# An attention and two mixtures of experts on one core: weights prepared later, gate terms on another engine, a state without zero blocks

## The chip, the cores and the metric

The kernel runs on 1 core of a Trainium2 chip. The metric is device time in microseconds (us): 711.42, the median of 3 runs (710.65 to 711.84). Five engines work in parallel, each through its own instructions in a fixed order: PE (TensorE, matrix products), DVE (VectorE), ACT (ScalarE), POOL (GpSimd) and SP (SyncE, which here only issues transfers). An instruction that waits holds up all that stand behind it on its engine.

## The reference, cut to what matters

```python
for t in range(S):                       # attention: B=2, H=8, S=768, D=40
    m_new  = max(f[t] + m, i[t])
    f_stab, i_stab = exp(f[t] + m - m_new), exp(i[t] - m_new)
    C = f_stab * C + i_stab * outer(v[t], k[t])
    n = f_stab * n + i_stab * k[t]
    y[t] = sigmoid(o[t]) * (C @ q[t]) / max(abs(n @ q[t]), 1)
x = y laid out as 1536 rows of 320
noisy = x @ w_gate + log1p(exp(x @ w_noise)) * noise       # 8 experts
out[r] = sum over r's two best experts of weight * (relu(x[r] @ w1[e]) @ w2[e])
final = sum over 4 experts of p[:, e] * (relu(out @ v1[e]) @ v2[e])
```

## The kernel before, in words

The attention goes in 12 chunks of 128 positions, 6 for each of the two batches. For a chunk, `o_S` (L346) makes the scores `sp` of keys and queries, `o_decay` (L323) makes a matrix `A` of decays on PE (`dp`), takes its exponent on ACT and masks it on POOL, `o_M` multiplies the two on DVE, and `o_AV` (L413) multiplies by the values into `hp`, on top of what `o_inter` (L402) put there from the running state `C` of the chunks before. ACT copies `hp` to `hs`, `o_tp` transposes it into `tp`, and `o_x` (L429) normalizes it on DVE and multiplies by the sigmoid of the output gate into `x`. `o_xp` transposes `x` again (`xp`, copied to `xt`), and `o_lg` makes the routing logits. The state is advanced by `o_Cg` (POOL, decay `gb`), `o_U` (PE, `up`, from the weighted keys `kw`) and `o_Cu` (DVE). `C` holds 4 pairs of heads in blocks of 105 columns: the two heads of a pair stand on rows 0 to 39 and 64 to 103, and the other two blocks are zero.

What `A` needs of the two gates is made along the whole sequence in four parts, chunk 0, chunk 1, chunks 2 and 3, chunks 4 and 5 (`PARTS`): `gates` (L246) does the scans on DVE, `gates_terms` (L260) forms the factors `tk` and `tq` of the decay's exponent, and `gates_turn` transposes the weights `awr`. `LFh` and `ash` are rounded copies that ACT makes for it. `sigmoid(b)` (L282) takes the sigmoid of a batch's output gates in one ACT instruction between two loads of ACT's function tables.

For each batch `route` (L479) places each row's two experts, in two halves (4 and 2 chunks), some 30 small DVE instructions each: `rh` and `oh` are the factors of the products `pt` (L551) that fill the table `tok`, from which POOL gathers (L616) the rows `xe` of an expert from `Xall` in DRAM. Then `moe1` works through the experts (hidden layer L207, second layer L221), and `moe2` does the four experts of the second mixture over all rows. A weight is loaded (`raw`, 4 buffers, L173) and split into a high part on ACT (L187) and a low part on DVE (L188), five quarters of `w1` and five of `w2` ahead of use.

The order on each engine comes from a scheduler that places an instruction when its model of the chip says the inputs are there; `tc.issue_after` puts instructions behind a given one. So splits written far down in the program are placed wherever an engine looked free. `PLAN1` says which pieces are written one after the other: `A` a piece of the attention (four a chunk), `r` and `q` a piece of the two halves of the routing, `l` a load of a weight, `w` a split and a load, `g` the second batch's sigmoid, `X` the first gathers, `P` the first expert's rows.

Of the kernel before, what the change touches and what calls it, by code (L numbers as in the profile page):

```python
# [65 lines left out]
def body(ctx: ExitStack, tc: tile.TileContext, d, o, dbg=None):  # L66
# [159 lines left out]


# [5 lines left out]
    fi_load(slice(0, 1))  # L233
# [26 lines left out]
    def gates_terms(part):  # L260

        n = PARTS[part]
        nc.scalar.copy(LFh[:, n], LF[:, n])
        nc.scalar.copy(ash[:, n], asr[:, n])
        nc.vector.tensor_scalar(flat(LF, n), flat(LF, n), low, keys, ALU.mult, ALU.add)
        nc.vector.scalar_tensor_tensor(flat(LF, n), flat(LFh, n).bitcast(F32), qsel, flat(LF, n), ALU.mult, ALU.add)
        nc.vector.tensor_scalar(flat(asr, n), flat(asr, n), key, sums, ALU.mult, ALU.add)
# [99 lines left out]
    def o_kw(i):  # L367
        b, c = divmod(i, NC)
        if c < NC - 1:
            kw = at2.tile([P, H, D], F32, name="kw")  # L370
            nc.vector.tensor_mul(kw, st[i]["kv"][:, :, 0:D], w_t[:, c, b * H : (b + 1) * H].unsqueeze(2).to_broadcast([P, H, D]))
            st[i]["kw"] = kw

    def o_Cg(i):
        c = i % NC
        if 0 < c < NC - 1:
            for j in range(2):
                r, e = slice(64 * j, 64 * j + 40), slice(64 * j, 64 * j + 41)
                nc.gpsimd.tensor_mul(Cs[1 - c % 2][r, :, e], Cs[c % 2][r, :, e], st[i]["gb"][r, :, P - 1 : P].to_broadcast([40, 4, 41]))

    def o_U(i):
        if i % NC < NC - 1:
            t = st[i]
            up = psum([104, 4, 41], "up")
            for p in range(4):
                for j in range(2):
                    nc.tensor.matmul(up[64 * j : 64 * j + 40, p, :], t["kw"][:, 4 * j + p, :], t["kv"][:, 4 * j + p, D:], start=True, stop=True)
            t["up"] = up

    def o_Cu(i):  # L390
        c = i % NC
        if c < NC - 1:
            up = st[i]["up"]
            for j in range(2):
                r = slice(64 * j, 64 * j + 40)
                cs = Cs[1 - c % 2][r, :, 64 * j : 64 * j + 41]
                if c == 0:
                    st[i]["cu"] = nc.vector.tensor_copy(cs, up[r]).ins
                else:
                    nc.vector.tensor_add(cs, up[r], cs)  # L400
# [44 lines left out]
    def o_xp(i):  # L445
# [485 lines left out]
    def splits():  # L931
        for _ in range(NQ):
            w_split()
            w_load()
            yield

    def follow(plan, b, first):
        r, q, f, w = route(b, 0), route(b, 1), routed_(b), splits()
        for group in plan.split():
            for t in group:  # L940
# [121 lines left out]
```

## Time and profile before

| | us |
|---|---|
| median of 3 runs | 711.42 |
| the profiled execution | 714.27 |
| its span | 712.5 |
| PE busy | 679.9 (95%) |
| DVE busy | 379.2 (53%) |
| ACT busy | 248.3 (35%) |
| POOL busy | 108.3 (15%) |
| start of the scores of chunks 1, 2, 3, 6, 7 | 18.14, 41.97, 51.85, 70.83, 79.09 |
| first rows of an expert on PE | 112.33 |

The span runs from the first to the last instruction; the remaining 1.8 us of the profiled execution lie around it. The busy share of PE counts an instruction for as long as it takes at the clock that it was granted.

### The profile page before, as it was taken

How to read it: one execution, taken by the hardware profiler on the slowest of the kernel's cores; microseconds unless marked ns; L12 is line 12 of the kernel's file. 1: busy time of each engine (PE TensorE's matmuls, PEld its weight loads, DVE VectorE, ACT ScalarE, POOL GpSimd, SP SyncE). 2: the span in 40 equal slices, each digit the busy share in tenths (PEclk: the TensorE clock that was granted, in tenths of full speed). 3: DMA queues.
4: the chain of work that ended last, by engine and by line, in shares of the span. 5: the costliest groups of instructions: out<-in, count | busy, mean ns of one | idle time of the engine just before them, and what ended most of it. 6: DMA issues, size and time to landing. Idle time of an engine off the chain costs nothing.

```text
span 712.5 us, 11304 instructions
## 1 busy us (share of the span) xinstructions
PE 679.9 (95%) x4448; PEld 618.6 (87%) x4448; DVE 379.2 (53%) x834; ACT 248.3 (35%) x439; POOL 108.3 (15%) x168
## 2 busy tenths in 40 slices
PE   7588889999999999999999999999999999999997
PEld 3367668999899999999989899898998998989987
DVE  7887876888465745747865525413344124332131
ACT  3638323554353534544541314202233023121120
POOL 4554433102222101014114000000000000000000
PEclk8569769999999999999999999999999999999999
DMA  8667433556465454467663003200031001001011
GB/s 259 193 181 211 132 76 88 172 181 199 131 193 158 139 163 126 133 180 246 199 193 100 1 1 104 59 1 1 19 107 38 1 1 37 1 1 38 1 37 40
DMA packets 36433, 73.78 MB, mean 104 GB/s; under 512 B 7576, under 2 KB 14744, under 8 KB 36376
## 3 DMA queue, kind: packets, MB, share of 16 engines
q1 hardware_dynamic: 33752, 64.16, 30.1%
q0 software_dynamic: 2624, 8.85, 4.3%
q8 instruction: 37, 0.61, 0.4%
q14 instruction: 20, 0.16, 0.1%
HBM read 64.07 MB, written 8.92 MB: 102 GB/s over the span
## 4 chain that ended last, share of the span: by engine, by line
PE 85%; DVE 7%; DMA 4%; ACT 1%; issue 1%; SPq 0%; ACTq 0%; DVEq 0%
PE z L207 24%; PE z L221 24%; PE s L207 13%; PE s L221 11%; DMA raw<-w 2%; PE sp L353 2%; PE hp L418 2%; PE lp L461 1%; PE s L217 1%; DVE w1lo L188 1%; DMA raw<-v 1%; PE hp L411 1%; DMA fi<-fi 1%; PE pa L630 1%; DVE hh L225 1%
## 5 line engine op out<-in xcount | busy, mean ns | idle before, releaser
L224 ACT ACTIVATE hh<-z 128x512 fp32r<-128x512 f32 x96 | 57.1, 600 | 190.7 <-PE z L207 189.4
L221 PE MATMUL z<-w2hi,hh 128*128 128x320 f32 x384 | 118.5, 309 | 0.0
L221 PE MATMUL z<-w2hi,hl 128*128 128x320 f32 x384 | 118.3, 308 | 0.0
L221 PE MATMUL z<-w2lo,hh 128*128 128x320 f32 x384 | 118.3, 308 | 0.0
L207 PE MATMUL z<-x2h,w1hi 128*128 128x512 f32 x288 | 112.4, 390 | 0.0
L221 PE MATMUL s<-w2hi,hh 128*128 128x320 f32 x448 | 107.8, 313 | 2.5 <-issue 1.2
L225 DVE SCALAR_TENSOR_TENSOR hl<-z,hh 128x512 fp32r<-128x512 f32 x96 | 65.7, 690 | 80.9 <-ACT hh L224 80.9
L207 PE MATMUL z<-x2h,w1lo 128*128 128x512 f32 x288 | 96.6, 389 | 0.0
L188 DVE TENSOR_TENSOR w2lo<-raw,w2hi 128x640 fp32r<-128x640 f32 x60 | 50.3, 841 | 68.3 <-ACT w2hi L187 64.3
L207 PE MATMUL s<-xh,w1hi 128*128 128x256 f32 (+1 forms) x288 | 85.3, 313 | 0.0
L221 PEld LDWEIGHTS s<-w2hi,hh 128*128 128x128 f32 x448 | 76.7, 188 | 4.3 <-issue 1.9
L207 PE MATMUL z<-x2l,w1hi 128*128 128x512 f32 x192 | 74.8, 390 | 0.0
L188 DVE TENSOR_TENSOR w1lo<-raw,w1hi 128x768 fp32r<-128x768 f32 x60 | 58.7, 979 | 29.4 <-ACT w1hi L187 28.9
L187 ACT CAST w2hi<-raw 128x640 fp32r<-128x640 f32 x60 | 43.8, 731 | 87.0 <-PE s L217 23.9
L221 PEld LDWEIGHTS z<-w2lo,hh 128*128 128x128 f32 x384 | 72.1, 188 | 0.6
L221 PEld LDWEIGHTS z<-w2hi,hh 128*128 128x128 f32 x384 | 72.1, 188 | 0.5
L221 PEld LDWEIGHTS z<-w2hi,hl 128*128 128x128 f32 x384 | 72.1, 188 | 0.0
L207 PE MATMUL s<-xh,w1lo 128*128 128x256 f32 (+1 forms) x288 | 70.6, 309 | 0.0
L221 PE MATMUL s<-w2lo,hh 128*128 128x320 f32 x224 | 69.2, 309 | 0.0
L187 ACT CAST w1hi<-raw 128x768 fp32r<-128x768 f32 x60 | 50.3, 838 | 48.7 <-PE s L207 23.8
L207 PEld LDWEIGHTS z<-x2h,w1lo 128*128 128x128 f32 x288 | 54.1, 188 | 11.3
L207 PEld LDWEIGHTS z<-x2h,w1hi 128*128 128x128 f32 x288 | 54.0, 188 | 10.8
(204 smaller groups left out, 1003.4 us busy)
## 6 DMA issues: line engine op xcount, KB each, us to landing
raw<-w SPq DMA_DIRECT2D x44, 384.0 KB
raw<-w SPq DMA_DIRECT2D x44, 320.0 KB
raw<-v SPq DMA_DIRECT2D x16, 384.0 KB
raw<-v SPq DMA_DIRECT2D x16, 320.0 KB
kv<-kv SPq DMA_DIRECT2D x12, 324.0 KB
Yd<-ys SPq DMA_DIRECT2D x8, 320.0 KB
kp<-kT SPq DMA_DIRECT2D x12, 208.0 KB
qt<-qT SPq DMA_DIRECT2D x12, 208.0 KB
```

Source lines behind the costliest of these rows:

```text
L187: nc.scalar.copy(hi, raw)
L188: nc.vector.tensor_sub(lo, raw, hi.bitcast(F32))
L207: nc.tensor.matmul(out_ps, l, r, start=(i == 0), stop=(i == len(seq) - 1))
L217: nc.tensor.matmul(yp, both[f], r[:, k], start=(f == 0 and i == 0), stop=(f == NF - 1 and i == 1))
L221: nc.tensor.matmul(yp, l, r, start=(f == 0 and i == 0), stop=(f == NF - 1 and i == 2))
L224: nc.scalar.activation(hh, src, AF.Relu)
L225: nc.vector.scalar_tensor_tensor(hl, src, 0.0, hh.bitcast(F32), ALU.max, ALU.subtract)
L353: nc.tensor.matmul(sp[g][:, j, :], t["kp"][r, j, :], t["qt"][r, j, :], start=True, stop=True)
L411: nc.tensor.matmul(hp[:, p, :], Cs[c % 2][:, p, :], t["qg"][:, p, :], start=(p == 0), stop=False)
L418: nc.tensor.matmul(hp[64 * j : 64 * j + 41, p, :], t["kv"][:, 4 * j + p, D:], t["A"][:, 4 * j + p, :], start=False, stop=(p == 3))
L461: nc.tensor.matmul(lp, xts[i % 2][:, k, :], wgn[:, k, : 2 * E1], start=(k == 0), stop=(k == 2))
L630: nc.tensor.transpose(pk[k][:, c], xe[:r, s, k * P : (k + 1) * P], ident[:r, :r])
```

## The change

The change has seven parts. The loads `l` and the splits `w` of `PLAN1` are put behind the newest transfer of `kv` (SP), exponent of a decay (ACT) and product with `A` (DVE) that were written before them, and the plan moves them later. The first sigmoid is put behind chunk 1's exponents, which no longer wait for it; the terms of gate part 2 are put behind it instead. In parts 1 to 3 of the gates, two DVE operations and the product `tq` of POOL become ACT instructions (`tq` in four pieces of 128 columns). `C` loses its zero blocks: one instruction where there were two in `o_Cg` and `o_Cu`, and eight small matrix products instead of four in `o_inter`. The narrow half of `xt` is copied by ACT instead of DVE. The gates' load is cut after two chunks instead of one. The routing gets one more break before the products `pt`, and the gathers `X` come one group sooner.

```diff
-PLAN1 = "A A A A A A Al A Al A Ag Al A Al A A Ar Ar Aw Ar Ar Aw Ar Ar Aqr Aqr Aq Aqr Aqw Aq Aq qwX Aq AF A AF A F P"
+PLAN1 = "A A A A A A A A Al A Ag Al A Al A Al Ar Ar Ar Ar Awr Ar Awr Ar Aqr Aqr Awq Aq Awq Aq Aq Aq qX Aq AF A F A F P"
+    front = {}
+    def behind():
+        stack = ExitStack()
+        for ins in front.values():
+            stack.enter_context(tc.issue_after(ins))
+        return stack
-    fi_load(slice(0, 1))
+    fi_load(slice(0, 2))
...
-        nc.vector.tensor_scalar(flat(LF, n), flat(LF, n), low, keys, ALU.mult, ALU.add)
+        if part == 0:
+            nc.vector.tensor_scalar(flat(LF, n), flat(LF, n), low, keys, ALU.mult, ALU.add)
+        else:
+            nc.scalar.activation(flat(LF, n), flat(LF, n), AF.Identity, scale=low, bias=keys)
...
-        eng = nc.vector if part == 0 else nc.gpsimd
         for c in range(n.start, n.stop):
...
+            else:
+                for j in range(4):
+                    nc.scalar.activation(tq[:, c, j], LF[:, c], AF.Identity, scale=head[:, j : j + 1])
...
-        C = at.tile([104, 4, 105], F32, name=f"C{i}")
+        C = at.tile([104, 4 * 41 + 24], F32, name=f"C{i}")
...
-            for j in range(2):
-                r, e = slice(64 * j, 64 * j + 40), slice(64 * j, 64 * j + 41)
-                nc.gpsimd.tensor_mul(Cs[1 - c % 2][r, :, e], Cs[c % 2][r, :, e], st[i]["gb"][r, :, P - 1 : P].to_broadcast([40, 4, 41]))
+            nc.gpsimd.tensor_mul(state(1 - c % 2), state(c % 2), st[i]["gb"][:, :, P - 1 : P].to_broadcast([104, 4, 41]))
...
-                nc.tensor.matmul(hp[:, p, :], Cs[c % 2][:, p, :], t["qg"][:, p, :], start=(p == 0), stop=False)
+                for j in range(2):
+                    r, m = slice(64 * j, 64 * j + D), 41 if j else 64
+                    nc.tensor.matmul(hp[64 * j : 64 * j + m, p, :], Cs[c % 2][r, 41 * p : 41 * p + m], t["qg"][r, p, :], start=(p == 0), stop=False)
...
-        nc.vector.tensor_copy(xt[0:DR, 2], xp[0:DR, 2])
+        nc.scalar.copy(xt[0:DR, 2], xp[0:DR, 2])
...
             nc.vector.tensor_mul(rh[:, 1, c], in_col[:, c], place[...])
         yield
+        yield
         pt = psum([P, 2, E1 * NCOL], "pt")
...
-    exps = sigmoid(0, st[-1]["exp"])
-    with tc.issue_after(exps):
-        for op in ("D0", "D1", "G", "S"):
-            do(op, 1)
+    for op in ("D0", "D1", "G", "S"):
+        do(op, 1)
+    exps = sigmoid(0, front["act"])
...
-    with tc.issue_after(last):
+    with tc.issue_after(last), tc.issue_after(exps):
         last = gates_terms(2)
...
     def splits():
         for _ in range(NQ):
-            w_split()
+            with behind():
+                w_split()
+                w_load()
+            yield
+
+    def behind_load():
+        with behind():
             w_load()
-            yield
```

On ACT, between the weights of chunk 1 (`w_t`) and the first weights of gate part 2, this stands in the kernel before (`x_91` is batch 0's output gate, `dp_330` and `dp_334` the decays of chunk 1):

```order
L280 ACTIVATE w_t<-pt_300 128x16
L284 ACT_TABLE_LOAD
L286 ACTIVATE x_91<-x_91 128x1920
L420 COPY hs<-hp_312 105x512
L288 ACT_TABLE_LOAD
L333 ACTIVATE A<-dp_330 128x512
L333 ACTIVATE A<-dp_334 128x512
L343 ACTIVATE gb<-gp_338 104x512
L263 CAST LFh<-LF 128x256
L264 CAST ash<-asr 128x256
L280 ACTIVATE w_t<-pt_373 128x16
L187 CAST w1hi<-raw 128x768
```

And from the exponents of chunk 1 on in the changed kernel (`tq` x8 are the factors of chunks 2 and 3):

```order
L350 ACTIVATE A<-dp_329 128x512
L350 ACTIVATE A<-dp_333 128x512
L360 ACTIVATE gb<-gp_337 104x512
L301 ACT_TABLE_LOAD
L303 ACTIVATE x_91<-x_91 128x1920
L305 ACT_TABLE_LOAD
L272 CAST LFh<-LF 128x256
L273 CAST ash<-asr 128x256
L277 ACTIVATE LF<-LF,mix,kind 128x256
L282 ACTIVATE asr<-asr,mix,kind 128x256
L297 ACTIVATE w_t<-pt_381 128x16
L289 ACTIVATE tq<-LF,head 128x128 x8
```

The exponents and `gb` of chunk 1 now stand before the sigmoid and its table loads, six or more new instructions before the exponents of chunk 2, and no split of a weight.

On DVE, in the second half of batch 0's routing up to `rh`, this stands before:

```order
L535 TENSOR_REDUCE sf_1198<-tmp_1197 128x4
L579 RECIPROCAL mx<-mx 128x6
L359 TENSOR_TENSOR A<-sp_1213,A 128x512
L534 TENSOR_TENSOR tmp_1197<-sel,sl_1143 128x32
L543 TENSOR_TENSOR in_col_1205<-count,sf_1198 128x128
L535 TENSOR_REDUCE sf_1198<-tmp_1197 128x4
L359 TENSOR_TENSOR A<-sp_1214,A 128x512
L541 TENSOR_TENSOR oh_1203<-count,sf_1198 128x512
L544 TENSOR_SCALAR rh_1204<-in_col_1205,place 128x128
L547 TENSOR_TENSOR rh_1204<-in_col_1205,place 128x64 x2
```

And in the changed kernel, in the same place:

```order
L596 TENSOR_TENSOR lk<-lk,mx 128x12
L188 TENSOR_TENSOR w2lo<-raw,w2hi 128x640
L555 TENSOR_REDUCE sf_1234<-tmp_1233 128x4
L598 TENSOR_TENSOR mx<-lk 128x6
L188 TENSOR_TENSOR w2lo<-raw,w2hi 128x640
L554 TENSOR_TENSOR tmp_1233<-sel,sl_1179 128x32
L563 TENSOR_TENSOR in_col_1241<-count,sf_1234 128x128
L555 TENSOR_REDUCE sf_1234<-tmp_1233 128x4
L599 TENSOR_SCALAR mx<-mx 128x6
L564 TENSOR_SCALAR rh_1240<-in_col_1241,place 128x128
L561 TENSOR_TENSOR oh_1239<-count,sf_1234 128x512
L567 TENSOR_TENSOR rh_1240<-in_col_1241,place 128x64 x2
```

Two of the low parts of `w2` now stand among the routing's instructions; the two products with `A` went ahead of this piece.

On PE, around the last product of that table (`up_1259`, `dp_1269` and `dp_1273` belong to chunks 10 and 11), before:

```order
L551 LDWEIGHTS oh_1203
L551 MATMUL pt_1239<-rh_1204,oh_1203 128x64
L387 MATMUL up_1259<-kv,kw 40x41 x7
L332 MATMUL dp_1269<-tq,tk 128x512
L332 MATMUL dp_1273<-tq,tk 128x512
L461 MATMUL lp_1282<-wgn,xt_189 128x16 x3
L426 MATMUL tp_1291<-ident,hs 128x105 x4
```

And now:

```order
L407 MATMUL up_1274<-kv,kw 40x41
L349 MATMUL dp_1284<-tq,tk 128x512
L349 MATMUL dp_1288<-tq,tk 128x512
L481 MATMUL lp_1297<-wgn,xt_189 128x16 x3
L572 LDWEIGHTS oh_1239
L572 MATMUL pt_1303<-rh_1240,oh_1239 128x64
```

The products for `up`, `dp` and `lp` stood behind those of the table and now stand ahead of them.

## Rows read from the trace of the kernel before

**Rows 1.** the page, its head and the engines' busy time
```profile
span 712.5 us, 11304 instructions
...
PE 679.9 (95%) x4448; PEld 618.6 (87%) x4448; DVE 379.2 (53%) x834; ACT 248.3 (35%) x439; POOL 108.3 (15%) x168
```

**Rows 2.** timeline of PE: start, us, engine, line, form, count [idle before <-releaser]
```profile
18.14 2.08 PE L353 MATMUL sp<-qt,kp 40*128 40x128 f32 x16
...
25.89 0.80 PE L332 MATMUL dp<-tq,tk 32*128 32x512 f32 x2 [2.98 <-POOL tq L272]
...
28.01 0.79 PE L332 MATMUL dp<-tq,tk 32*128 32x512 f32 x2
32.90 0.45 PE L279 MATMUL pt<-ident,awr 128*128 128x128 f32 x1 [4.09 <-DVE awr L257]
...
36.38 1.58 PE L418 MATMUL hp<-A,kv 128*41 128x128 f32 x16
41.14 0.69 PE L449 MATMUL xp<-ident,x 128*128 128x128 f32 x2 [3.17 <-DVE x L439]
...
41.97 2.08 PE L353 MATMUL sp<-qt,kp 40*128 40x128 f32 x16
...
51.85 1.16 PE L353 MATMUL sp<-qt,kp 40*128 40x128 f32 x16
```

**Rows 3.** timeline of ACT to 62 us
```profile
11.36 0.30 ACT L263 CAST LFh<-LF 128x128 fp32r<-128x128 f32 x1 [1.66 <-DVE LF L254]
...
14.23 1.81 ACT L286 ACTIVATE x<-x 128x1920 f32<-128x1920 f32 x1
...
18.84 1.28 ACT L288 ACT_TABLE_LOAD   x1
...
24.08 0.83 ACT L187 CAST w1hi<-raw 128x768 fp32r<-128x768 f32 x1 [1.69 <-DMA raw<-w]
...
30.06 1.08 ACT L333 ACTIVATE A<-dp 128x512 f32<-128x512 f32 x2
```

**Rows 4.** timeline of DVE to 62 us
```profile
32.67 2.03 DVE L188 TENSOR_TENSOR w1lo<-raw,w1hi 128x768 fp32r<-128x768 f32 x1
...
52.60 0.94 DVE L188 TENSOR_TENSOR w1lo<-raw,w1hi 128x768 fp32r<-128x768 f32 x1
...
55.30 0.33 DVE L400 TENSOR_TENSOR C<-up,C 40x164 f32<-40x164 f32 x1
...
58.56 0.28 DVE L453 COPY xt<-xp 64x128 f32<-64x128 f32 x1 [1.29 <-ACT xt L452]
```

**Rows 5.** timeline of POOL
```profile
24.69 2.40 POOL L272 TENSOR_TENSOR tq<-LF,head 128x512 fp32r<-128x512 f32 x2 [0.43 <-DVE LF L266]
...
104.07 1.18 POOL L616 DMA_INDIRECT xe<-Xall,tok  x1 [6.14 <-DVE wdense L584]
```

**Rows 6.** windows: stretch, us, each engine busy (instructions), clock, DMA share, GB/s
```profile
40.00:50.00 10.00, 8.86 (x60) 7.25 (x62) 8.29 (x18) 3.82 (x8) 3.89 (x5) 0.54 0.81 240
50.00:60.00 10.00, 10.00 (x129) 8.05 (x126) 7.11 (x20) 7.39 (x12) 5.61 (x7) 0.94 0.75 227
...
80.00:90.00 10.00, 7.18 (x102) 5.81 (x98) 9.80 (x41) 3.15 (x8) 3.94 (x5) 0.93 0.46 139
90.00:100.00 10.00, 8.01 (x68) 6.42 (x64) 8.11 (x38) 2.93 (x7) 3.56 (x5) 0.73 0.38 95
```

**Rows 7.** timeline of PE from 59 us
```profile
70.35 0.44 PE L449 MATMUL xp<-ident,x 128*128 128x128 f32 x2 [1.99 <-DVE x L439]
...
70.83 1.42 PE L353 MATMUL sp<-qt,kp 40*128 40x128 f32 x16
...
79.09 1.16 PE L353 MATMUL sp<-qt,kp 40*128 40x128 f32 x16
...
101.53 0.23 PE L551 MATMUL pt<-rh,oh 128*128 128x64 bf16 x2 [3.52 <-DVE rh L547]
...
112.33 0.42 PE L630 MATMUL pa<-ident,xe 128*128 128x128 f32 x2
```

More of the change, by code (lines that the diff above doesn't have):

```diff
@@ L264, in gates_terms @@
         nc.scalar.copy(ash[:, n], asr[:, n])
-        nc.vector.tensor_scalar(flat(LF, n), flat(LF, n), low, keys, ALU.mult, ALU.add)
+        if part == 0:
+            nc.vector.tensor_scalar(flat(LF, n), flat(LF, n), low, keys, ALU.mult, ALU.add)
+        else:
+            nc.scalar.activation(flat(LF, n), flat(LF, n), AF.Identity, scale=low, bias=keys)
         nc.vector.scalar_tensor_tensor(flat(LF, n), flat(LFh, n).bitcast(F32), qsel, flat(LF, n), ALU.mult, ALU.add)
-        nc.vector.tensor_scalar(flat(asr, n), flat(asr, n), key, sums, ALU.mult, ALU.add)
+        if part == 0:
+            nc.vector.tensor_scalar(flat(asr, n), flat(asr, n), key, sums, ALU.mult, ALU.add)
+        else:
+            nc.scalar.activation(flat(asr, n), flat(asr, n), AF.Identity, scale=key, bias=sums)
         keep = nc.vector.scalar_tensor_tensor(flat(tk, n), flat(ash, n).bitcast(F32), ksel, flat(asr, n), ALU.mult, ALU.add)
-        eng = nc.vector if part == 0 else nc.gpsimd
         for c in range(n.start, n.stop):
-            wide = lambda x: x.unsqueeze(1).to_broadcast([P, 4, P])
-            last = eng.tensor_mul(tq[:, c], wide(LF[:, c]), head.unsqueeze(2).to_broadcast([P, 4, P]))
+            if part == 0:
+                last = nc.vector.tensor_mul(tq[:, c], LF[:, c].unsqueeze(1).to_broadcast([P, 4, P]), head.unsqueeze(2).to_broadcast([P, 4, P]))
+            else:
+                for j in range(4):
+                    nc.scalar.activation(tq[:, c, j], LF[:, c], AF.Identity, scale=head[:, j : j + 1])
         return last.ins if part == 0 else keep.ins
@@ L313, in o_load @@
             kv = at2.tile([P, H, 2 * D + 1], F32, name="kv", bufs=3)
-            nc.sync.dma_start(kv, d["kv"][b, c])
+            front["sp"] = nc.sync.dma_start(kv, d["kv"][b, c]).ins
             t["kv"] = kv
@@ L369, in o_kw, with state @@
         if c < NC - 1:
-            kw = at2.tile([P, H, D], F32, name="kw")
-            nc.vector.tensor_mul(kw, st[i]["kv"][:, :, 0:D], w_t[:, c, b * H : (b + 1) * H].unsqueeze(2).to_broadcast([P, H, D]))
+            kw = at2.tile([P, H * D], F32, name="kw")
+            nc.vector.tensor_mul(kw.rearrange("t (h d) -> t h d", h=H), st[i]["kv"][:, :, 0:D], w_t[:, c, b * H : (b + 1) * H].unsqueeze(2).to_broadcast([P, H, D]))
             st[i]["kw"] = kw
+    def state(k):
+        return Cs[k][:, : 4 * 41].rearrange("r (p e) -> r p e", p=4)
     def o_Cg(i):
@@ L386, in o_U @@
                 for j in range(2):
-                    nc.tensor.matmul(up[64 * j : 64 * j + 40, p, :], t["kw"][:, 4 * j + p, :], t["kv"][:, 4 * j + p, D:], start=True, stop=True)
+                    h, m = (4 * j + p) * D, D if j else 64
+                    nc.tensor.matmul(up[64 * j : 64 * j + m, p, :], t["kw"][:, h : h + m], t["kv"][:, 4 * j + p, D:], start=True, stop=True)
             t["up"] = up
@@ L393, in o_Cu @@
             up = st[i]["up"]
[L394 to L400, printed above, removed]
+            cs = state(1 - c % 2)
+            if c == 0:
+                nc.vector.tensor_copy(cs, up)
+            else:
+                nc.vector.tensor_add(cs, up, cs)
     def o_inter(i):
@@ L873, in body @@
     o_load(0, ("qt",))
-    fi_load(slice(1, NC))
+    fi_load(slice(2, NC))
     o_load(0, ("kv",))
@@ L948, in follow @@
                 else:
-                    {"l": w_load, "P": lambda: prep(first), "g": lambda: sigmoid(1, st[-1]["exp"])}[t]()
+                    {"l": behind_load, "P": lambda: prep(first), "g": lambda: sigmoid(1, front["act"])}[t]()
             yield
```

6 lines of the change are left out of this document (3 added, 3 removed).

## The prediction

> **What bounds the kernel now.** I read the page first: PE is busy for 679.9 us of a span of 712.5 [rows 1], so the end moves by what PE waits, and by what it works at the lower clock. Second, the timeline of PE, for its gaps. They lie in the first 102 us; from the last long one, 3.52 us before 101.53 [rows 7], the following work runs nearly without a stop, and the first expert's rows reach PE at 112.33 [rows 7]. What moves that point moves the end. Third, the stretch with the greatest loss: the scores of chunk 1 start at 18.14, those of chunk 2 at 41.97, those of chunk 3 at 51.85 [rows 2]. PE idles 2.98 us for POOL's `tq`, 4.09 for DVE's `awr` and 3.17 for DVE's `x` [rows 2]. The granted clock is 0.54 (mostly 1.2 GHz) from 40 to 50 us and 0.94 from 50 to 60 [rows 6], and the same scores take 2.08 us at 41.97 and 1.16 at 51.85 [rows 2]: here a wait costs twice. Last, the timelines of ACT, DVE and POOL say who is late. ACT sits in the sigmoid and the table load behind it until 20.12, then waits 1.69 us for a weight at 24.08 and brings chunk 2's exponents only at 30.06, though their product started at 25.89 [rows 2, 3]. DVE takes 2.03 us for a split at 32.67 that takes 0.94 at 52.60 [rows 4]. POOL needs 2.40 for a pair of `tq` [rows 5].
>
> **Chunk 1 to chunk 2, the first term.** The product `dp` of chunk 1 now stands behind all eight of `hp`, so I put the scores of chunk 1 at 18.6 instead of 18.14, and the exponents and `gb`, which no longer wait for the sigmoid, end at about 19.7. Table load, sigmoid and table load are 1.28 + 1.81 + 1.28 = 4.4 [rows 3]: 24.1. Then come four instructions of gate part 2 (`LFh`, `ash`, `LF`, `asr`) on 256 columns, for which the 0.30 of 128 columns [rows 3] is the floor and twice that the ceiling; at 0.38 they end at 25.6. The first four `tq` are of 128 columns: by the 0.30 apiece 1.2, with the overlap that lets two exponents of 512 pass in 1.08 [rows 3] nearer 1.0. So chunk 2's `dp` starts at 26.6, later than 25.89 before. But what follows on PE then has nothing left to wait for: to the end of chunk 3's `dp`, 28.80 - 25.89 = 2.9; from `pt` at 32.90 to the end of `hp` at 37.96, 5.1, less 0.3 for a `pt` and 0.6 for three of eight products that now come later; and 0.8 from `xp` to the scores [rows 2]. That is 7.9, and the scores of chunk 2 start at 34.5. `awr` is ready in time, since the split, the two DVE operations on `LF` and `asr` and POOL's load on DVE are gone from ahead of it. I allow half a microsecond for what I can't see: 35.0, a gain of 7.0. The bounds: 33.9 with `tq` at 0.2 apiece; 36.2 if `prob`, whose reduction now stands ahead of `asr` on DVE, lands as late as the weight whose place in the queue it takes (24.08) [rows 3], since then part 2's remaining DVE work ends 1.1 later than I have it.
>
> Here a rule is weighed. Two exponents of 128x512 took 1.08 us, so about 0.5 for a further one [rows 3]; no row has an ACT instruction with a scale from memory. The Trainium skill (ScalarE: Activation LUTs, What ACT_TABLE_LOAD costs) says that each operand of one value a row adds about 93 ns. By it the four first `tq`, `LF` and `asr` would cost an estimated 0.7 more before chunk 2, and the first term would be 6.3 instead of 7.0.
>
> **Chunk 2 to chunk 3.** Before, 51.85 - 41.97 = 9.9, with PE working throughout, mostly at 1.2 GHz [rows 2, 6]. If the clock stays there the stretch takes 10.5 (three products of `hp` came in); at 2.4 GHz it takes 9.9 x 1.16 / 2.08 = 5.5, plus 0.4. Before 50 us PE had worked since 41.14 without a gap before the clock came back; now it works without one from 26.6. So part of the stretch, I take half, runs at 2.4 GHz: 8.5, a gain of 1.4, bounds -0.6 and 4.0. Scores of chunk 3 at 43.5 instead of 51.85.
>
> **To chunk 7.** The gap of 1.99 before 70.35 goes to `x`, with a split just ahead of it on DVE that now is gone; from 70.83 to 79.09 PE works mostly at 1.2 GHz after that gap, 8.3 us for a chunk [rows 7]. Two splits come in before `x` of chunk 6 is stored and the next begins, and the merged `C` and the copy of `xt` go. I count 1.8, bounds 0 and 3.5.
>
> **Routing, a loss.** DVE is busy 9.80 and 8.11 of 10 us from 80 to 100 [rows 6]. Between the scores of chunk 7 and the last `rh` six splits now stand that stood at 27 to 50 us: at about 0.88 (0.94 for one of `w1` [rows 4], somewhat less for `w2`) 5.3 us. Out of it go three updates of half of `C` at 0.33 and three copies of `xt` at 0.28 [rows 4]: 1.8. Net 3.5 later. Bounds: 1.6 if the 2.1 us that DVE idles there take up 1.9 of it, and 10.4 if each split costs the 2.03 of the worst row [rows 4], since POOL works here too. On SP a load of `w2` waits for a split to free its buffer, and behind it wait keys, queries and values of the next chunks; I count nothing, as they are loaded a chunk ahead.
>
> **The gather.** From `pt` at 101.53 to the expert's rows at 112.33 PE worked for 10.8 us [rows 7]. Some 3 us of it, `up`, `dp` and `lp`, now stand ahead of `pt` and fill part of the wait for `rh`. But rows are not there sooner for that: behind `tok` POOL issues four gathers of some 1.2 us, 104.07 to 109 [rows 5]. So PE reaches `xe` early, and the gather is late next. One more split of 0.8 stands ahead of `tok`; the mask of `A` now comes before the gathers instead of 5 us after. I take 0.8 lost, bounds -1 and 4 (a gap there lowers the clock for the first expert).
>
> **The rest.** `C` merged saves POOL and DVE time that nothing else waits for. The eight products of `o_inter` use separate rows and columns of the array, as the scores use separate rows: 16 passes of 128 columns took 1.16 us [rows 2]. So I count nothing; one after the other they would take 0.9 more a chunk at most. In the trace the products of `hp` by halves of the columns follow at 1.58 for 16 at a mixed clock [rows 2], with no sign of a gap. The Trainium skill (TensorEngine Tiling (Array Packing), Tiling Modes) says that a change of the tiling mode drains the engine; `o_inter` now is in a mode of its own. [...] The other gates' load costs 0.4 at the first scan and gives back as much at the second. Experts and second mixture have the same instructions, and take part by the shift alone.
>
> **Sum.** -7.0 - 1.4 - 1.8 + 3.5 + 0.8 = -5.9. The profiled execution took 714.27 (span 712.5 [rows 1] and 1.8 around it), so its like would be 708.4. The median of the runs, 711.42, is 2.9 below that execution; I take the difference over: 705.5.
>
> **Rivals.**
> *All of it arrives.* With the bounds on the good side in the first 80 us (7.4, 3.0 and 2.5) and DVE's idle time taking up the splits (1.6 lost), 11.3 are gained: 700.1. For it: PE's gaps before 42 us alone are 10.2 us [rows 2]. Against it: DVE is full where the splits go [rows 6].
> *The gain is given back.* The attention gains 8.4 by chunk 3, but with splits at 1.2 us, between the 0.94 and the 2.03 [rows 4], routing loses 5.5, the gather 3, and nothing is kept at chunk 6: no change, 711.5. For it: the wait for `rh` is already the last one before the experts [rows 7].
> *Slower.* Splits at 2.03 each, in DVE's queue ahead of `x` and `rh` and in turn with POOL's masks, lose 10.4 in routing, and the gather 3, against 8.4: 716.4. It decides from the point where the last `rh` is ready later than 101.53. Against it: only one of the rows of splits shows this price, and POOL then had `tq`, which it loses.
> *It doesn't happen.* That the scheduler puts the splits early all the same is excluded: their places on DVE are behind chunk 6.
>
> **How the numbers follow.** Forecast 0.54, all of it 0.17, given back 0.15, slower 0.14. The forecast's own range, from its bounds taken half together, is 701.5 to 710. The range of 8 in 10 goes from 699.5, just past the first rival, to 714, into the slower one. A measurement here tells 0.2% (1.4 us) from no change. Faster by more: the first two cases and a little of the third, 0.72. Within: most of the third and the forecast's edge, 0.13. Slower: 0.15.
>
> **What would show it.** Scores of chunk 2 near 35 and of chunk 3 near 43.5; no gap over 1 us on PE between chunk 2's `dp` and its scores; no wait of ACT for `raw` before 60 us; a clock at 2.4 GHz before 42 us; six splits of 0.8 to 1.2 us between the scores of chunk 7 and `rh`; `rh` at about 97 and the first rows of the expert near 107. I am wrong if the scores of chunk 2 come after 38 (then ACT's queue or `prob` is the bound), or if they come at 35 and the expert still starts at 112 (then routing eats the gain).

## The result, and the profile after

The changed kernel takes 718.98 us (median of 4 runs, 718.11 to 722.89) where the kernel before took 711.63 in the same runs: a ratio of 1.0113, with a 95% interval of 1.0072 to 1.0154 (it is formed from all the runs; the two medians alone would give 1.0103). Ratios, intervals and medians of clocks leave out the few runs over 1.5% above the fastest of their kernel: three of e3's twelve, three of e6's eleven, two of e10's eleven, one each of e7's, e8's and e9's twelve, and one of the kernel before. It is slower by 1.1%; I had forecast 705.5 and a range up to 714. The profiled execution took 719.56.

The head of the page of the changed kernel, for [rows 1]:

```profile
span 717.8 us, 11459 instructions
...
PE 690.1 (96%) x4528; PEld 625.2 (87%) x4528; DVE 367.1 (51%) x806; ACT 258.1 (36%) x477; POOL 95.3 (13%) x155
```

PE is busy 10.2 us longer and the span is 5.3 us longer. PE has 80 more instructions, four more products of `inter` in two passes each on ten chunks, but the time is not theirs alone. The timeline of PE of the changed kernel to 70 us, for [rows 2] (start, us, engine, line, form, count, idle before):

```profile
27.10 0.80 PE L349 MATMUL dp<-tq,tk 32*128 32x512 f32 x2 [0.79 <-ACT tq L289]
...
36.77 0.79 PE L370 MATMUL sp<-qt,kp 40*128 40x128 f32 x2
...
37.90 2.07 PE L370 MATMUL sp<-qt,kp 40*128 40x128 f32 x14
...
49.18 1.16 PE L370 MATMUL sp<-qt,kp 40*128 40x128 f32 x16
...
60.04 0.58 PE L446 MATMUL tp<-ident,hs 105*128 105x105 f32 x4 [1.61 <-ACT hs L440]
```

The same view of it from 60 us, for [rows 7]:

```profile
76.92 0.41 PE L469 MATMUL xp<-ident,x 128*128 128x128 f32 x2 [2.45 <-DVE g L542]
...
77.37 1.16 PE L370 MATMUL sp<-qt,kp 40*128 40x128 f32 x16
...
106.32 0.40 PE L572 MATMUL pt<-rh,oh 128*128 128x64 bf16 x4 [3.30 <-DVE rh L567]
...
116.73 0.67 PE L651 MATMUL pa<-ident,xe 128*128 128x128 f32 x2
```

The first scores of chunk 2 start 5.2 us sooner than before, the rest 4.1. Those of chunk 3 start at 49.18, only 2.7 sooner, and those of chunk 7 at 77.37, only 1.7. The last `pt` comes at 106.32, 4.8 later, and the experts' first rows at 116.73, 4.4 later. So the gain arrives in the first part, shrinks from 37 us on, and turns into a loss between chunk 7 and the experts. The windows of the changed kernel, for [rows 6] (stretch, us, busy PE, PEld, DVE, ACT, POOL, granted clock, DMA share, GB/s):

```profile
30.00:40.00 10.00, 9.45 (x56) 6.67 (x56) 5.40 (x12) 6.26 (x19) 5.00 (x6) 0.50 0.05 17
40.00:50.00 10.00, 10.00 (x82) 7.89 (x84) 2.95 (x10) 2.97 (x7) 2.96 (x4) 0.57 0.32 94
...
100.00:110.00 10.00, 6.70 (x51) 5.18 (x51) 8.78 (x39) 2.83 (x6) 2.87 (x4) 0.50 0.69 217
110.00:120.00 10.00, 10.00 (x80) 8.88 (x80) 4.71 (x13) 3.35 (x8) 5.86 (x7) 0.50 0.53 150
```

Here is the surprise: from 30 to 50 us PE works 19.45 of 20 us, and the granted clock stays at 0.50 to 0.57 (1.2 GHz). At the end it is low again, 0.50 from 100 to 120, and in the last of these windows PE worked without a break. Before, PE at 110 to 120 us ran at 1.00:

```profile
110.00:120.00 10.00, 10.00 (x115) 9.00 (x116) 6.95 (x18) 4.17 (x9) 4.34 (x6) 1.00 0.28 72
```

From 17 to 125 us the mean clock is 0.70 against 0.76 before.

The timeline of its ACT (for [rows 3]), where the gate terms cost what I had put:

```profile
20.89 1.80 ACT L303 ACTIVATE x<-x 128x1920 f32<-128x1920 f32 x1
...
24.00 0.41 ACT L272 CAST LFh<-LF 128x256 fp32r<-128x256 f32 x1
...
24.62 0.60 ACT L277 ACTIVATE LF<-LF,mix,kind 128x256 f32<-128x256 f32 x1
...
25.77 2.44 ACT L289 ACTIVATE tq<-LF,head 128x128 fp32r<-128x128 f32 x8
```

The sigmoid ends where I had it, and eight `tq` take 2.44, the 0.30 apiece of the rows. `LF` with two operands takes 0.60, a cast of the same size 0.41: 0.095 for each operand. With this the trace agrees with the Trainium skill (ScalarE: Activation LUTs, What ACT_TABLE_LOAD costs), whose 93 ns I had left out of the sum.

The timeline of its DVE (for [rows 4]), the splits in the routing:

```profile
74.64 1.74 DVE L188 TENSOR_TENSOR w1lo<-raw,w1hi 128x768 fp32r<-128x768 f32 x1
...
104.08 0.82 DVE L188 TENSOR_TENSOR w2lo<-raw,w2hi 128x640 fp32r<-128x640 f32 x1
...
106.04 0.35 DVE L567 TENSOR_TENSOR rh<-in_col,place 128x64 bf16<-128x64 bf16 x2
```

Six stand around and behind the scores of chunk 7, the first just ahead of these scores at 76.80 and five behind them; they take 0.81 to 0.95 each, 5.3 in all, as expected, and the last of them, at 104.08, stands 2 us ahead of the last `rh`. One behind chunk 6, at 74.64, takes 1.74.

### The profile page after: what moved, and what is told of

It reads as the page before. It is cut to its first block, busy times and chain, and to the rows that moved or that the text cites. A ratio compares the mean times of both kernels' runs of the same rounds, so it can differ in the third digit from the quotient of the medians.

```text
span 717.8 us, 11459 instructions
## 1 busy us (share of the span) xinstructions
PE 690.1 (96%) x4528; PEld 625.2 (87%) x4528; DVE 367.1 (51%) x806; ACT 258.1 (36%) x477; POOL 95.3 (13%) x155
## 4 chain that ended last, share of the span: by engine, by line
PE 82%; DMA 7%; DVE 6%; issue 1%; ACT 1%; SPq 1%; ACTq 0%; DVEq 0%
PE z L207 24%; PE z L221 24%; PE s L207 12%; PE s L221 10%; DMA raw<-w 3%; DMA kv<-kv 2%; PE hp L438 2%; PE hp L431 2%; PE sp L370 2%; PE s L217 1%; DVE w1lo L188 1%; PE lp L481 1%; DMA raw<-v 1%; DMA prob<-prob 1%; PE pa L651 1%
## 5 line engine op out<-in xcount | busy, mean ns | idle before, releaser
L187 ACT CAST w2hi<-raw 128x640 fp32r<-128x640 f32 x60 | 43.5, 728 | 84.2 <-PE s L217 25.1
L207 PEld LDWEIGHTS z<-x2h,w1hi 128*128 128x128 f32 x288 | 54.1, 188 | 10.8
```

Source lines behind the costliest of these rows:

```text
L187: nc.scalar.copy(hi, raw)
L207: nc.tensor.matmul(out_ps, l, r, start=(i == 0), stop=(i == len(seq) - 1))
```

## The experiments

Two theories. *W*: the state without zero blocks makes narrow products (`inter` on 40 rows in eight pieces; and `up`, whose weights for the first head of each pair go from 40 to 64 columns, which the section on the change does not say); they take longer on PE, and PE gets 1.2 GHz for longer beside them. *S*: the splits and the plan cost in the routing what the attention gains. Ratios are to the kernel before, run in turn on the same chip, with 95% intervals; "clock" is the mean granted clock of the span, the median over a kernel's runs (before: 0.957 to 0.959 in every group; the changed kernel: 0.951).

| run | ratio | interval | clock |
|---|---|---|---|
| e1 changed, zero blocks | 1.0021 | 0.9998 to 1.0043 | 0.956 |
| e2 before, narrow state | 1.0141 | 1.0102 to 1.0180 | 0.948 |
| e3 changed, old plan | 1.0009 | 0.9983 to 1.0036 | 0.951 |
| e4 before, gate terms | 1.0026 | 1.0002 to 1.0049 | 0.963 |
| e5 changed, zero blocks, old plan | 0.9969 | 0.9938 to 0.9999 | 0.961 |
| e6 before, `inter` split | 1.0082 | 1.0049 to 1.0116 | 0.944 |
| e7 before, `up` wide | 1.0011 | 0.9980 to 1.0043 | 0.958 |
| e8 e1, splits earlier | 1.0005 | 0.9968 to 1.0042 | 0.960 |
| e9 before, `inter` doubled | 1.0033 | 1.0008 to 1.0059 | 0.965 |
| e10 before, `inter` split, 104 rows | 1.0057 | 1.0034 to 1.0081 | 0.955 |
| e11 e5, a wait filled | 0.9973 | 0.9949 to 0.9997 | 0.969 |
| e12 e5, two waits filled | 0.9953 | 0.9927 to 0.9979 | 0.970 |

### e1: the zero blocks back

```diff
-        C = at.tile([104, 4 * 41 + 24], F32, name=f"C{i}")
+        C = at.tile([104, 4, 105], F32, name=f"C{i}")
...
-                for j in range(2):
-                    r, m = slice(64 * j, 64 * j + D), 41 if j else 64
-                    nc.tensor.matmul(hp[64 * j : 64 * j + m, p, :], Cs[c % 2][r, 41 * p : 41 * p + m], t["qg"][r, p, :], ...)
+                nc.tensor.matmul(hp[:, p, :], Cs[c % 2][:, p, :], t["qg"][:, p, :], ...)
```

> The changed kernel with the state C kept in blocks of 105 columns with zeros, four products an `inter` and `up` of 40 rows, as before; all else as changed. Theory W (narrow products): the eight products of `inter` and the wider `up` take longer on PE (in the changed kernel 1.89 instead of 1.57 and 1.00 instead of 0.70 us at 1.2 GHz), and in their company the granted clock stays at 1.2 GHz from 17 to 49 us and from 92 to 120 us; with the old state the clock comes back 8 to 9 us after a gap as before, the scores of chunk 3 start by 46 and the time is 711 or less. Theory S (splits in the routing): the state only gives back what its products cost directly, some 0.5 us on ten chunks, and the time is 714 to 716, with `rh` as late as in the changed kernel (106).

The timeline of PE of this run:

```profile
37.14 1.16 PE L370 MATMUL sp<-qt,kp 40*128 40x128 f32 x16
...
42.92 1.16 PE L370 MATMUL sp<-qt,kp 40*128 40x128 f32 x16
...
73.42 1.67 PE L370 MATMUL sp<-qt,kp 40*128 40x128 f32 x16
...
103.03 0.40 PE L569 MATMUL pt<-rh,oh 128*128 128x64 bf16 x4 [5.17 <-DVE rh L564]
```

The scores of chunk 3 start at 42.92, my 43.5, and from 37.14 to 50 us each takes 1.16 us: the clock is back, where the changed kernel got it at 49. So W holds up to here. But the ratio is 1.0021, and W alone had it at 1.000 or less: of 5.7 us gained at chunk 7 nothing is left at the last `pt`, which waits 5.17 for `rh`, as S has it. And with whole products, too, the clock is low for long in one place, from 74 to 94 us; one of its windows:

```profile
80.00:90.00 10.00, 9.23 (x77) 6.94 (x77) 7.90 (x25) 2.90 (x8) 3.60 (x5) 0.50 0.36 103
```

### e2: the narrow state alone

```diff
-        C = at.tile([104, 4, 105], F32, name=f"C{i}")
+        C = at.tile([104, 4 * 41 + 24], F32, name=f"C{i}")
...
+                    h, m = (4 * j + p) * D, D if j else 64
+                    nc.tensor.matmul(up[64 * j : 64 * j + m, p, :], t["kw"][:, h : h + m], ...)
...
+                    nc.tensor.matmul(hp[64 * j : 64 * j + m, p, :], Cs[c % 2][r, 41 * p : 41 * p + m], t["qg"][r, p, :], ...)
```

> The kernel before with the state without zero blocks alone (one instruction in `Cg` and `Cu`, eight products in `inter`, `up` of 64 rows). Theory W: slower by 4 us or more, 715 to 720, with stretches at 1.2 GHz that are longer than the 8 to 9 us of before. Theory S: within 2 us of before, at most 713.5.

1.4% slower, 725.68 us, more than W expected (the kernel before took 714.76 on this chip). The timeline of PE of this run, for its gaps:

```profile
42.97 0.69 PE L452 MATMUL xp<-ident,x 128*128 128x128 f32 x2 [2.56 <-DVE x L442]
...
76.79 1.17 PE L353 MATMUL sp<-qt,kp 40*128 40x128 f32 x16
```

Its window from 50 to 70 us:

```profile
50.00:70.00 20.00, 20.00 (x150) 15.12 (x146) 9.55 (x23) 10.03 (x14) 4.88 (x6) 0.50 0.40 108
```

Between the gap at 42.97 and the scores at 76.79 PE has no gap that the rows show, and it works at 1.2 GHz for nearly all of these 34 us. Before, the gap at 41.14 was followed by 2.4 GHz in the scores at 51.85 [rows 2].

### e3: the plan of before

```diff
+PLAN1 = "A A A A A A Al A Al A Ag Al A Al A A Ar Ar Aw Ar Ar Aw Ar Ar Aqr Aqr Aq Aqr Aqw Aq Aq qwX Aq AF A AF A F P"
...
-            with behind():
-                w_split()
-                w_load()
+            w_split()
+            w_load()
...
-        yield
```

> The changed kernel with the loads and splits of weights, the plan and the route's breaks as before: the splits stand at 25 to 70 us again and none is tied. Theory W: still slower than before, 716 or more. Theory S: the routing has its splits no longer, the last `pt` comes 5 us sooner than in the changed kernel, and the time is 712 or less.

The timeline of PE of e3:

```profile
79.06 2.08 PE L370 MATMUL sp<-qt,kp 40*128 40x128 f32 x16
...
102.13 0.23 PE L571 MATMUL pt<-rh,oh 128*128 128x64 bf16 x2 [2.49 <-DVE rh L567]
```

e3 also takes back the plan of the second batch's pieces (`PLAN2`), which the change had altered beside `PLAN1`. The median of all twelve is 716.61, but against the kernel before on the same chip the ratio is 1.0009: 1.0% comes back, with the narrow state still there. From the scores of chunk 7 to the last `pt` it takes 23.1 us, in the changed kernel 29.0; the last `pt` comes 4.2 sooner, near the 5 of S. S holds as well; W's "still slower" can't be told from the noise. The clock is as low as in the changed kernel.

### e4: the gate terms alone

```diff
+                    nc.scalar.activation(tq[:, c, j], LF[:, c], AF.Identity, scale=head[:, j : j + 1])
...
-    exps = sigmoid(0, st[-1]["exp"])
-    with tc.issue_after(exps):
-        for op in ("D0", "D1", "G", "S"):
-            do(op, 1)
+    for op in ("D0", "D1", "G", "S"):
+        do(op, 1)
+    exps = sigmoid(0, st[-1]["exp"])
```

> The kernel before with the gate terms on ACT and the first sigmoid behind chunk 1's exponents, nothing else. Both theories: the scores of chunk 2 start 3 to 5 us sooner than 41.97 and the time is 706 to 710; my forecast's first term by itself. If the gain is lost before the first expert, 711 to 712.

The timeline of PE of e4:

```profile
39.27 1.16 PE L361 MATMUL sp<-qt,kp 40*128 40x128 f32 x16
...
45.69 1.16 PE L361 MATMUL sp<-qt,kp 40*128 40x128 f32 x16
...
86.70 0.39 PE L559 MATMUL pt<-rh,oh 128*128 128x64 bf16 x4 [4.64 <-DVE rh L555]
...
102.58 0.23 PE L559 MATMUL pt<-rh,oh 128*128 128x64 bf16 x2 [3.84 <-DVE rh L555]
```

The scores of chunk 2 come 2.7 us sooner (3 to 5 were expected), those of chunk 3 6.2, and nothing is left of it: the first `pt` waits 4.64 for `rh` and starts at 86.70, half a microsecond sooner than before; the second is 1.0 later than before, and so are the experts' rows. The forecast of a gain was wrong here. What came is the case "if the gain is lost" and a little worse: 1.0026 is slower than before by its interval, if barely.

### e5: zero blocks and the plan of before

The edits of e1 and e3 together.

> The changed kernel with the state in blocks with zeros and with the plan, the loads and splits and the route's breaks as before; what is left of the change is the gate terms on ACT, the later sigmoid, the copy of `xt` and the gates' load. Theory W (the narrow products hold the clock at 1.2 GHz) with S (the splits in the routing cost what the attention gains): both losses are out, and the ratio is 0.990 to 0.996. Rival R: what the attention gains is lost at the routing's first `rh` and at the second sigmoid whatever stands there, as in the run with the gate terms alone: 1.000 to 1.003.

The timeline of PE of e5:

```profile
72.54 1.53 PE L370 MATMUL sp<-qt,kp 40*128 40x128 f32 x16
...
81.73 0.39 PE L568 MATMUL pt<-rh,oh 128*128 128x64 bf16 x4 [3.50 <-DVE rh L564]
...
97.84 0.29 PE L568 MATMUL pt<-rh,oh 128*128 128x64 bf16 x2 [2.98 <-DVE rh L564]
...
109.73 0.41 PE L647 MATMUL pa<-ident,xe 128*128 128x128 f32 x2
```

0.3% faster than before, just outside the expected 0.996. With both losses out, the attention is 6.5 us ahead at chunk 7, but two waits for `rh` with a low clock behind each leave 2.6 at the experts' rows. The ratio lies between what the two theories gave, so the rival R holds in part.

### e6, e7, e10, e9: which of the narrow products, and what of it

e6 splits `inter` alone, out of the blocks of before; e10 does the same on all rows:

```diff
-                nc.tensor.matmul(hp[:, p, :], Cs[c % 2][:, p, :], t["qg"][:, p, :], ...)
+                for j in range(2):
+                    r, m = slice(64 * j, 64 * j + D), 41 if j else 64
+                    nc.tensor.matmul(hp[64 * j : 64 * j + m, p, :], Cs[c % 2][r, p, 64 * j : 64 * j + m], t["qg"][r, p, :], ...)
```

> The kernel before with `inter` alone in eight products of 40 rows out of the same blocks of C; `up`, `Cg` and `Cu` as before. If the products of `inter` hold the clock, PE works on at 1.2 GHz for 15 us and more behind a gap, and the ratio is 1.010 to 1.016 like that of the narrow state. If `up` holds it, the clock comes back after 8 to 9 us, and the ratio is at most 1.004 (0.3 us on ten chunks).

e7 widens `up` alone:

```diff
-                    nc.tensor.matmul(up[64 * j : 64 * j + 40, p, :], t["kw"][:, 4 * j + p, :], ...)
+                    h, m = (4 * j + p) * D, D if j else 64
+                    nc.tensor.matmul(up[64 * j : 64 * j + m, p, :], t["kw"][:, h : h + m], ...)
```

> The kernel before with `up` alone widened to 64 columns for the first head of a pair; `inter`, `Cg` and `Cu` as before. If the products of `inter` hold the clock: at most 1.004 (0.1 to 0.3 us on ten chunks), and the clock comes back 8 to 9 us after a gap. If `up` holds it: 1.010 or more.

In e10, with the rows of `C` and `qg` not cut:

```diff
-                    nc.tensor.matmul(hp[64 * j : 64 * j + m, p, :], Cs[c % 2][r, p, 64 * j : 64 * j + m], t["qg"][r, p, :], ...)
+                    nc.tensor.matmul(hp[64 * j : 64 * j + m, p, :], Cs[c % 2][:, p, 64 * j : 64 * j + m], t["qg"][:, p, :], ...)
```

> The kernel before with `inter` in eight products of 64 and 41 columns, as in the run that split it, but each on all 104 rows of C. Theory W1, rows: the clock comes back 8 to 10 us after a gap, and the ratio is at most 1.005. Theory W1, columns or the number of products: as the run that split it into 40 rows, 1.006 to 1.011, with stretches at 1.2 GHz of 15 us and more.

e9 leaves `inter` whole and adds work:

```diff
                 nc.tensor.matmul(hp[:, p, :], Cs[c % 2][:, p, :], t["qg"][:, p, :], ...)
+                nc.tensor.matmul(hp[:, p, :], Cz[:, p, :], t["qg"][:, p, :], ...)
```

> The kernel before with a second product of full size (104 rows, 105 columns) behind each of the four of `inter`, on a state of zeros: eight products as in the narrow state, with more work on PE than these, but on all rows. Theory W1 (it is the few rows and columns of the narrow products that keep the clock at 1.2 GHz): the clock comes back 8 to 10 us after a gap as before, and the ratio is 1.002 to 1.007 (0.8 us on ten chunks at most, part of it in waits). Rival W2 (any added work on PE moves its waits and so the clock): 1.008 or more, with stretches at 1.2 GHz of 15 us and more.

The window from 110 to 120 us, behind the last `pt` of batch 0 (at 104.52, 101.31 and 104.12 us), of e6, of e10 and of e9 in this order:

```profile
110.00:120.00 10.00, 10.00 (x74) 7.99 (x71) 3.14 (x10) 1.80 (x5) 5.28 (x7) 0.50 0.23 68
```

```profile
110.00:120.00 10.00, 10.00 (x125) 8.63 (x124) 6.31 (x17) 3.61 (x9) 4.55 (x6) 0.98 0.26 68
```

```profile
110.00:120.00 10.00, 10.00 (x114) 9.00 (x113) 5.31 (x18) 3.46 (x8) 6.14 (x8) 1.00 0.45 119
```

PE works without a break in all three; with 40 rows at 1.2 GHz, with 104 at 2.4. The split of `inter` is most of the narrow state (1.0082, clock 0.944), though less than the 1.010 to 1.016 that I had expected of it; the wide `up` is nothing that can be told (1.0011). With 104 rows the ratio is 1.0057, between my two cases (at most 1.005 for rows, 1.006 to 1.011 for the number of pieces), and its interval overlaps that of e6: by the times alone rows and number of pieces can't be told apart.

What tells them apart is the clock over many runs: 0.941 to 0.956 in e6's eight runs, 0.949 to 0.960 in e10's nine, 0.959 to 0.971 in e9's eleven (e6 ran on another chip than e10 and e9, but the kernel before has the same 0.957 to 0.959 on both). A single trace doesn't. The profiled execution of e7, with `inter` whole, is at 1.2 GHz for 30 us, from 72 to nearly 102, where I had expected 8 to 9 us (its clock of 0.947 is not typical of its runs, 0.958), and e1 has its 20 us.

Then the direct cost. The products of `inter` of one chunk and the instruction that follows them, in the kernel before and in e6:

```profile
54.90 1.04 PE L411 MATMUL hp<-qg,C 104*105 104x128 f32 x8
55.69 0.47 PE L341 MATMUL gp<-tq,over 128*104 128x512 f32 x1
```

```profile
55.13 1.08 PE L413 MATMUL hp<-qg,C 40*64 40x128 f32 x16
56.15 0.47 PE L341 MATMUL gp<-tq,over 128*104 128x512 f32 x1
```

From start to start, eight pieces take 1.02 us where four whole products took 0.79 (at 2.4 GHz), and 1.89 where they took 1.57 (at 1.2). The `tp` just ahead of them takes 0.49 instead of 0.40, and 0.87 instead of 0.73. That is 0.3 to 0.5 us a chunk, 3 to 5 on ten, or 0.4 to 0.6%: it covers all of e10's 1.0057, and the 0.5 us on ten chunks that the expectation for e1 gave theory S was far too little. What the 40-row products cost beyond that goes with the lower clock. This is argued from the clocks above; no run changes the clock alone. e9 bears on the other rival, that any added work does it: it adds 0.9 to 1.0 us a chunk on full rows, costs 2.4 us in all, and its clock is higher than before, 0.965. Added work alone does not lower it.

### e8: the splits earlier

```diff
-PLAN1 = "A A A A A A A A Al A Ag Al A Al A Al Ar Ar Ar Ar Awr Ar Awr Ar Aqr Aqr Awq Aq Awq Aq Aq Aq qX Aq AF A F A F P"
+PLAN1 = "A A A A A A Al Al Al Al Agw Aw Aw Aw Aw A Ar Ar Ar Ar Ar Ar Ar Ar Aqr Aqr Aq Aq Aq Aq Aq Aq qX Aq AF A F A F P"
```

> The changed kernel with the state in blocks with zeros, and with the five tied splits and the loads put earlier in the plan: on DVE four low parts behind the products with `A` of chunk 4 and three behind those of chunk 5, one between those of chunk 8 and of chunk 9, where the run with zero blocks had two behind chunk 5 and six later. Theory S: the routing loses 3 us or more less than there, the last `pt` starts by 100 instead of 103, and the ratio is 0.992 to 0.997. Rival R: the splits then stand in the way of `x` of chunks 5 and 6, the gaps there drop the clock, and the ratio stays at 1.000 to 1.004.

The timeline of PE of e8:

```profile
64.81 0.66 PE L466 MATMUL xp<-ident,x 128*128 128x128 f32 x2 [2.37 <-DVE nl L512]
...
98.14 0.23 PE L569 MATMUL pt<-rh,oh 128*128 128x64 bf16 x2 [2.68 <-DVE rh L564]
```

The scores of chunk 2 start at 35.07. The ratio can't be told from 1, nor from e1's, so this doesn't separate S from R. The profile shows both: the last `pt` at 98.14, 4.9 sooner than in e1, as S had it, and a new wait of 2.37 at 64.81 with 1.2 GHz behind it. The experts' rows, at 105.91, come 6.4 us sooner than before, the end only 2.0: PE then waits 2.6 in all for nothing that the profile shows at the second layer near 180 us (before: 1.2), with a clock of 0.83 there, and 0.8 for `xl`.

### e11, e12: the waits filled

```diff
+        if b == 0 and h == 1:
+            fill = psum([P, 4 * P], "fill")
+            with tc.issue_after(front["pe"]):
+                for i in range(12):
+                    nc.tensor.matmul(fill, zero[:, :P], zero, start=(i == 0), stop=(i == 11))
         pt = psum([P, 2, E1 * NCOL], "pt")
```

> The run with zero blocks and the plan of before, and twelve products of 128x512 on zeros in front of the second `pt`, behind the scores of chunk 9: work of 2.6 us that fills PE's last long wait before the experts (2.98 us there). If a wait costs by the clock behind it: the clock stays at 2.4 GHz behind that `pt`, the first expert's rows come 3 to 5 us sooner after it (11.9 us there), and the ratio is 0.990 to 0.994. If the rows come when POOL's gathers are done, whatever PE does: 0.996 to 0.998.

The timeline of PE of e11, then those of its DVE and of its POOL:

```profile
94.43 2.76 PE L570 MATMUL fill<-zero 128*128 128x512 bf16 x12
97.77 0.35 PE L573 MATMUL pt<-rh,oh 128*128 128x64 bf16 x4 [0.57 <-DVE rh L564]
...
105.21 0.41 PE L652 MATMUL pa<-ident,xe 128*128 128x128 f32 x2
...
109.86 0.58 PE L207 MATMUL s<-xl,w1hi 128*128 128x256 f32 x1 [2.44 <-DVE xl L200]
```

```profile
108.01 0.32 DVE L417 TENSOR_TENSOR C<-up,C 40x164 f32<-40x164 f32 x1 [2.98 <-POOL C L396]
```

```profile
107.52 1.00 POOL L396 TENSOR_TENSOR C<-C,gb 40x164 f32<-40x164 f32 x2
```

The clock stays up behind `pt`, and the rows of the experts reach PE 7.4 us behind `pt` instead of 11.9 in e5. And still the ratio is that of e5, 0.9973: `xl`, whose `xh` ACT has ready at 106.6, stands on DVE behind the update of `C`, which waits for the decay of `C` on POOL, and this stands behind four gathers, a mask and `qg`. PE waits 2.44 for it. The wait is moved, not gone.

e12 has twelve more in front of the first `pt`, behind `dve`'s newest product with `A`:

```diff
-        if b == 0 and h == 1:
+        if b == 0:
             fill = psum([P, 4 * P], "fill")
-            with tc.issue_after(front["pe"]):
+            with tc.issue_after(front["pe"] if h else front["dve"]):
```

> As the run with the filled gap, and twelve more such products behind `inter` of chunk 7, in front of its product with the values and of the first `pt` (a wait of 3.5 to 4.8 us for `rh` there). If the waits of the routing cost by the clock behind them: 2.4 GHz behind the first `pt` too, the scores of chunk 9 start 3 to 4 us sooner after those of chunk 8 than the 10 us there, and the ratio is 0.989 to 0.995. If DVE's chain to the last `rh` is the bound by then: that `rh` comes as late as before, and the ratio stays at 0.996 to 0.998.

The timeline of PE of e12:

```profile
85.72 0.47 PE L573 MATMUL pt<-rh,oh 128*128 128x64 bf16 x8 [1.64 <-DVE rh L564]
...
86.48 1.68 PE L370 MATMUL sp<-qt,kp 40*128 40x128 f32 x16
```

0.9953, at the edge between the two expectations, and the fastest of all: 709.03 us against 712.16, 0.5% faster than before and, by the two ratios, 1.6% faster than the changed kernel. It can't be told from e11. The profiled execution, at 712.29 and a clock of 0.962, is among the slowest of its runs (704.37 to 712.50). In it the first `pt` still waits 1.64 and the clock still falls (the scores at 86.48 take 1.68), so the gain at chunk 9 that I had put there is not in this trace.

## Why the prediction was wrong

**The step that failed** is in "The rest": of the eight products of `o_inter` I said that they use separate rows and columns "as the scores use separate rows", and counted nothing. The rows said the opposite, had I divided. Eight passes of the whole products take 0.79 (54.90 to 55.69 before), 0.10 apiece; 16 passes of the scores take 1.16, 0.07 apiece, over the same 128 columns. Had two of these run side by side, a pair would have taken 0.14, longer than one whole pass. They ran in turn, and so did the pieces of `inter`: 16 in 1.02, 0.06 apiece. Directly that costs 0.3 to 0.5 us a chunk. For the rest I had no term at all: beside products on 40 rows PE gets a lower clock (0.944 in e6 against 0.955 in e10 and 0.965 in e9). The narrow state costs 0.9% in the changed kernel (to e1, give or take 0.5%), 1.4% in the kernel before (e2) and 0.4% with the old plan (e3 to e5, not clear of noise).

This is not the whole miss of 13.5 us: 0.9% is 6.6. With zero blocks (e1) the ratio is still 1.002 and not my 0.992, since a second term, routing, was put too low.

**Chunk 1 to chunk 2** was right in mechanism: exponents before the sigmoid, sigmoid to 24.0, no wait for a weight. `dp` starts at 27.10 instead of 26.6. The scores come at 36.77 instead of 35.0: PE waits 0.55 for `awr` (30.85), which I had ready in time, `up` takes 1.00 instead of 0.70, `inter` and the `tp` ahead of it 0.4 longer, and `hp` is at 1.2 GHz to its end. With zero blocks it was 37.14 (e1) and 35.07 (e8), so 35.0 was in reach.

**Chunk 2 to chunk 3**: I took half of the stretch at 2.4 GHz. With zero blocks it was all of it, 5.8 us (e1), with the narrow state almost none, 12.4 from the first scores of chunk 2. The sign "2.4 GHz before 42 us" came at 49.

**To chunk 7** I had counted a gain of 1.8; it was a loss of 1.0 (28.2 us against 27.2): PE waits 1.61 for `hs` behind the second sigmoid on ACT and 2.45 before `xp`, where the split of 1.74 stands in DVE's queue ahead of `x`.

**Routing** I had mis-sized: from the scores of chunk 7 to the last `pt` it is 6.5 us more than before, not 3.5, within my bounds of 1.6 and 10.4. The window of this stretch, in the changed kernel and then in the kernel before:

```profile
77.37:106.32 28.95, 23.49 (x216) 18.31 (x215) 24.33 (x86) 12.73 (x29) 8.68 (x10) 0.65 0.51 153
```

```profile
79.09:101.53 22.44, 16.10 (x176) 13.14 (x175) 20.28 (x86) 6.59 (x17) 7.69 (x11) 0.85 0.42 114
```

DVE is busy for 4.0 us more, near my 3.5: the splits cost 0.81 to 0.95 each, as put. But it also idles 2.5 us more, where I had left its idle time as it was: it waits 1.22 for `tp`, 1.47 for `pt` and 0.63 for `sp` of PE, and 1.20 for `lk` of ACT. PE's clock is lower here, 0.65 against 0.85; how much of the 2.5 comes of that no run shows. The narrow state isn't needed for it: with zero blocks the stretch takes 29.6 at a clock of 0.62 (e1). Without plan and splits it takes 23.1 (e3).

**The gather** came out near the number, 10.4 from `pt` to the experts instead of 10.8 and 0.8 more, but not by what I had described. PE did not reach `xe` early to wait there: it worked at 1.2 GHz without a break from 106.32 to 116.73, and the last of the four gathers was issued at 112.66.

**The rivals.** "Slower" is what came, with 716.4 for it; but I had it from splits at 2.03 each, and that price is not what decided. Its other condition, that the last `rh` be later than 101.53, held. My 0.15 for a slower kernel was too little also because "given back" holds even without the two losses: e4 and e5 gain 6 us by chunk 3 and keep nothing and 2.6 of it at the experts' rows. The forecast's own range was too narrow by its own terms, too: the bounds of the five terms on the bad side add up to 15 us, 720.6, and half of that gives 713, not 710. And "All of it arrives" took 7.4, 3.0 and 2.5 where the terms' own bounds are 8.1, 4.0 and 3.5. Of the two signs that I had named for being wrong, the second came in substance: the scores of chunk 2 were well before 38, and the experts later than 112, so routing ate the gain.

What stays open: which part of the plan costs the 0.5% to 1.0% (the splits' place, the tying of the loads or the route's break) was not taken apart, since e8 can't be told from e1 or from before; and what PE waits for near 180 us.

## What to carry to other kernels

Before cutting zero blocks out of a product, count passes: half-size products that run in turn cost more PE time than whole ones with zeros, and here PE's mean clock was lower beside them. A gain at the start counts only from the place where the next engine's chain ends; follow the chain (here DVE's routing, then POOL's gathers and what stands behind them) to the last wait, and price each wait with the clock that follows it. Change the parts of such an edit one at a time: three of these seven (the state, the loads and splits with their plan, the break in the route) cost 1.4% together and hid 0.3% of gain.

## What the runs showed of the hardware

- PE at work from 42.97 to 76.79 us without a gap in the rows, at a granted clock of 0.50 (1.2 GHz) up to 70 us (e2). In the kernel before, four stretches at 1.2 GHz ended 8 to 10 us behind the gap ahead of them (41.14, 70.35, 87.24 and 101.53), and I had expected the same elsewhere. But e1 and e7, with whole products, have stretches of 20 and 30 us.
- Four more products a chunk on full rows raised the mean clock to 0.965 and cost 2.4 us, a quarter of their own time (0.9 to 1.0 us a chunk at 2.4 GHz) (e9).
- The runs of one kernel spread with the clock: 34 runs of the kernel before on one chip took 712.1 to 720.3 us, at a mean clock of 0.963 in the fastest and 0.952 in the slowest. With a dozen runs of each, the intervals here still reach 0.24% to 0.31% to either side.
